# Loading and transposing the first k and q by chunks of 128 tokens, with the opening of a fused attention and FFN kernel reordered

## The chip, the cores and the metric

The kernel runs on one core of a Trainium2 chip. The metric is device time in microseconds (us), the median of several runs. A core has five engines with queues of their own: TensorE (PE; its weight loads are listed as PEld), VectorE (DVE), ScalarE (ACT), GpSimd (POOL) and SyncE (SP). They meet only at semaphores. SyncE, ScalarE and GpSimd can each issue DMAs; GpSimd's go through a queue of their own kind (software descriptors), which here also casts float32 to bfloat16 on the way.

## The reference

Sliding-window causal attention (window 64, 8 batches, 8 heads, 576 tokens, head size 64), its heads put side by side to a 4608 x 512 matrix x, and a gated FFN on it:

```python
scores = (1.0 / np.sqrt(D)) * np.matmul(q, k.transpose(0, 1, 3, 2))
rel = pos[:, None] - pos[None, :]
mask = (rel >= 0) & (rel < 64)
attn = softmax(np.where(mask, scores, -1e9))
x = np.matmul(attn, v)              # -> (B*S, H*D) = (4608, 512)
g = x @ w_gate                      # 512 -> 1536
out = (g * sigmoid(g)) * (x @ w_val) @ w_out   # 1536 -> 512
```

Inputs and output are float32; the kernel works in bfloat16 with float32 accumulation.

## The kernel before

The 4608 tokens are cut into 36 chunks of 128. Attention goes by chunk, the FFN by groups of four chunks (512 tokens): `F` computes tiles of 128 of the 1536 hidden columns (matmuls with Wg, a tanh on ScalarE, matmuls with Wv, two VectorE instructions), `O` multiplies by w_out and stores. Attention of later chunks is threaded between the FFN's matmuls. The order of all work is written out by hand in `build`; a small graph class turns reads and writes of named tiles into semaphore waits, and every engine runs its instructions in the order in which `build` names them.

Only the opening is touched: chunks 0 to 3, which nothing can hide.

- `first_loads` (L801) loads k and q of chunks 0 and 1 together (256 tokens) as float32. Partition p holds, for one of four pairs of heads and one group of eight tokens, 2 KB per head of the pair. Each tensor takes two DMAs, one for the even heads (e0 = 0, from SyncE) and one for the odd (e0 = 1, from ScalarE), each 256 KB over all 128 partitions.
- `first_cast` (through `copy`, L260 on ScalarE, L261 on VectorE) casts to bfloat16, by halves e0.
- `first_T` (L827; L825 for chunks 2 and 3) transposes on TensorE, eight transposes for one tensor, into one PSUM bank. `first_ev` copies one chunk out of that bank into kT or qT.
- `next_load` (L808, GpSimd) loads k or q of chunks 2 and 3 with a cast; it is gated on VectorE's `init_nmask` (L304). `load` (L330) loads v of one chunk, `load_w` (L345) columns of Wg or Wv; `W(a, b)` calls it for both.
- `warm` (L847) runs dummy float32 matmuls on a zeroed tile `wz`, which VectorE sets first (L264).
- `Sa`/`Sbias` (L420) puts the additive mask of a chunk into two PSUM banks, `So` (L439) adds the scores and takes the exponentials on ScalarE (L447, two per chunk). `AVa`/`AVs` (L607) is the product with v, `AVn` (L623, L626) the division by the row sums on VectorE. `Xp` (L784) transposes the result on TensorE and, called with an engine, copies it to xT. `shift` makes copies of v moved by 64 partitions.
- `Fp` (L888 matmuls, L869 tanh, L874 and L876 VectorE) is `F` in steps; its first call takes tokens 0 to 255, so it needs xT of chunks 0 and 1.

PSUM banks are given out least recently used first (`bank`, `pair`).

Of the kernel before, what the change touches and what calls it, by code (L numbers as in the profile page):

```python
# [17 lines left out]
BF = dt.bfloat16  # L18
F32 = dt.float32
# [134 lines left out]
class _Kernel:  # L154
# [111 lines left out]
    def init(self):  # L266
        g = self.g
        self.zero(self.tri[:, :], ["tri"], 1.0)
        self.zero(self.wz[:, :], ["wz"])
        self.zero(self.ident[:, :], ["ident"])  # L270
        self.zero(self.wup[:, :], ["wup"])
        self.zero(self.qT[:, :, 128 * self.ZQ:], ["qpad"])
# [1 line left out]
        t = self.tri  # L274
# [500 lines left out]
    def Xp(self, n, kind="a"):  # L775
# [16 lines left out]

        return ev

    def first_loads(self):
        for x, src in (("k", self.k), ("q", self.q)):
            f, fkeys, _, _ = self.first[x]
            for e0, eng in ((0, "sp"), (1, "act")):
                a = src[0, e0::2, 0:256, :].rearrange("c (g j) d -> g c (j d)", j=8)
                d = f[:, e0].rearrange("p j d -> p (j d)")  # L800
                self.g.op(eng, lambda e, d=d, a=a: e.dma_start(d, a), reads=fkeys, writes=[("f", x, e0)], dma=True)  # L801

    def next_load(self, x, st=1, gate=None):
        d, keys = self.first[x, 1]
# [2 lines left out]
        d = d.rearrange("p j e d -> p e j d").rearrange("p e j d -> p e (j d)")  # L807
        self.g.op("pool", lambda e: e.dma_start(d, a), writes=keys, dma=True, after=gate)  # L808

    def first_cast(self, x, parts):  # L810
        f, fkeys, c, ckeys = self.first[x]
        for e0, j0, j1, eng in parts:
            self.copy(eng, c[:, j0:j1, e0, :], f[:, e0, j0:j1, :], [("f", x, e0)] + fkeys, [("fc", x, e0, j0)])
            self.first[x, 0] = self.first.get((x, 0), []) + [("fc", x, e0, j0)]

    def first_T(self, x, st=0):
        c, ckeys = self.first[x, 1] if st else (self.first[x][2], self.first[x][3] + self.first[x, 0])
        bank, bk = self.bank("a")
        tb = bank.bitcast(BF).rearrange("p (j t) -> p j t", j=8)

        def pe(e):
            for j in range(8):
                if st:
                    for p in range(2):
                        r = e.transpose(tb[64 * p:64 * p + 64, j, :], c[:, j, p, :], self.ident[:, :])  # L825
                else:
                    r = e.transpose(tb[:, j, :], c[:, j, :, :], self.ident[:, :])  # L827
            return r

        self.g.op("pe", pe, reads=["ident"] + ckeys, writes=[bk])  # L830
        return bank, bk

    def first_ev(self, x, n, eng, b, after=None):
        bank, bk = b
        dst = self.kT if x == "k" else self.qT
        g = 16 * (n % 2)
        a = bank.bitcast(BF).rearrange("p (j g c) -> p c g j", j=8, c=4)[:, :, g:g + 16, :]
        d = dst[:, :, 128 * n:128 * n + 128].rearrange("p c (g j) -> p c g j", j=8)
        return self.copy(eng, d, a, [bk], [(x + "T", n, 0), (x + "T", n, 1)], after)

    def warm(self, count):
        bank, bk = self.bank("a")
        z = self.wz[:, :].bitcast(F32)

        def pe(e):
            for _ in range(count):
                r = e.matmul(bank[:, 0:224], z[:, 0:128], z[:, 0:224], start=True, stop=True)  # L847
            return r

        self.g.op("pe", pe, reads=["wz"], writes=[bk])  # L850

    def Fp(self, c, fs, lo=0, hi=512, side=False):
        g = self.g
# [109 lines left out]
    def loads(self):  # L963
# [56 lines left out]
    def build(self):  # L1020
# [4 lines left out]
        self.warm(5)  # L1025
        self.first_cast("k", ((0, 0, 8, "dve"), (1, 0, 8, "act")))
        self.first_cast("q", ((0, 0, 8, "dve"), (1, 0, 5, "dve"), (1, 5, 8, "act")))
        fk = self.first_T("k")
        self.first_ev("k", 0, "dve", fk)
        fq = self.first_T("q")  # L1030
        q0 = self.first_ev("q", 0, "act", fq)
        s0 = self.Sa(0, True)
        self.first_ev("k", 1, "dve", fk)
        self.first_ev("q", 1, "dve", fq, q0)
        s1 = self.Sa(1, True)
        self.So(s0)
        fk = self.first_T("k", 1)
        self.first_ev("k", 2, "dve", fk)
        self.So(s1)
        self.first_ev("k", 3, "dve", fk)  # L1040
        s2 = self.Sa(2, True)
        fq = self.first_T("q", 1)
        self.first_ev("q", 2, "act", fq)
        self.first_ev("q", 3, "act", fq)
        self.early_loads()
        s3 = self.Sa(3, True)
        a0 = self.AVa(0)
        self.AVs(a0)
        self.So(s2)
        self.shift(1, 0, "dve")  # L1050
        self.shift(1, 1, "dve")
        self.AVn(a0)
        a1 = self.AVa(1)
        self.AVs(a1)
        self.So(s3)
        x0 = self.Xp(0)
        self.AVn(a1)
        a2 = self.AVa(2)
        self.AVs(a2)
        self.AVn(a2)  # L1060
        x0("act")
        x1 = self.Xp(1)
        x1("act")
        a3 = self.AVa(3)
        self.AVs(a3)
        x2 = self.Xp(2)
        f0 = self.Fp(0, (0, 1), 0, 256)
        f0("Wg", 0)
        f0("Wg", 1)
        x2("act")  # L1070
        self.AVn(a3)
        x3 = self.Xp(3)
        f0("tan", 0)
        x3("dve")
# [20 lines left out]
        fk = self.first_T("k", 1)  # L1095
        self.held.add(fk[1][1])
        fq = self.first_T("q", 1)
# [61 lines left out]
        for c in range(2, NFC):  # L1159
            for u in range(4):  # L1160
                n = 4 * c + u + 4
# [78 lines left out]
```

## Time and profile before

| | us |
|---|---|
| median of 3 runs | 326.02 (325.84 to 326.12) |
| the profiled execution, its own time | 326.52 |
| its span | 324.8 |
| PE busy | 319.2 (98% of the span) |
| DVE, ACT, POOL busy | 215.8, 125.8, 104.2 |
| DMA traffic | 39.83 MB moved, mean 123 GB/s |

The profile is of one execution. The span runs from its first instruction to its last; the time of an execution is 1.7 us longer. Times in the timeline and in the chain of waits are counted from the span's start. Line numbers are those of the kernel before. In a timeline row the bracket gives the idle time of the engine ahead of the row and what ended it; rows of one line that follow each other are merged, with their count. The DMA view gives for each issue the median time from issue to landing.

### The profile page before, as it was taken

How to read it: one execution, taken by the hardware profiler on the slowest of the kernel's cores; microseconds unless marked ns; L12 is line 12 of the kernel's file. 1: busy time of each engine (PE TensorE's matmuls, PEld its weight loads, DVE VectorE, ACT ScalarE, POOL GpSimd, SP SyncE). 2: the span in 40 equal slices, each digit the busy share in tenths (PEclk: the TensorE clock that was granted, in tenths of full speed). 3: DMA queues.
4: the chain of work that ended last, by engine and by line, in shares of the span. 5: the costliest groups of instructions: out<-in, count | busy, mean ns of one | idle time of the engine just before them, and what ended most of it. 6: DMA issues, size and time to landing. Idle time of an engine off the chain costs nothing.

```text
span 324.8 us, 7717 instructions
## 1 busy us (share of the span) xinstructions
PE 319.2 (98%) x3278; PEld 162.4 (50%) x3278; DVE 215.8 (66%) x400; ACT 125.8 (39%) x224; POOL 104.2 (32%) x134
## 2 busy tenths in 40 slices
PE   6999999999999999999999999999999999999996
PEld 5665565564544454545454444545454544444444
DVE  5886866688485966676768585958576767555510
ACT  3935563634332443333333242424242422222311
POOL 6999831142626061607060607060402000000000
DMA  7999999999999899959998998999687202000012
GB/s 189 179 191 186 205 172 167 161 150 149 158 138 167 128 100 137 163 109 152 119 115 122 146 141 81 146 132 163 71 110 96 69 32 67 32 34 32 32 67 97
DMA packets 154354, 39.83 MB, mean 123 GB/s; under 512 B 140368, under 2 KB 149328, under 8 KB 154320
## 3 DMA queue, kind: packets, MB, share of 16 engines
q0 software_dynamic: 104896, 18.36, 72.8%
q1 hardware_dynamic: 43952, 11.15, 24.7%
q10 hardware_dynamic: 5472, 9.83, 9.5%
q8 instruction: 26, 0.43, 0.5%
q14 instruction: 8, 0.07, 0.1%
HBM read 37.75 MB, written 9.44 MB: 145 GB/s over the span
## 4 chain that ended last, share of the span: by engine, by line
PE 96%; DMA 1%; ACT 1%; DVE 0%; SPq 0%; issue 0%
PE ps L888 58%; PE ps L930 29%; PE ps L692 2%; PE ps L514 2%; DMA hT<-in_q_dram 1%; PE ps L464 1%; PE ps L825 1%; ACT pt L447 1%; PE ps L382 1%; PE ps L420 1%; PE ps L582 1%; PE ps L468 0%; DVE ost L261 0%; PE ps L784 0%; PE ps L439 0%; ACT xT L260 0%
## 5 line engine op out<-in xcount | busy, mean ns | idle before, releaser
L874 DVE SCALAR_TENSOR_TENSOR uu<-sig,ps 128x512 bf16<-128x512 bf16 x108 | 73.9, 685 | 57.3 <-ACT sig L869 57.1
L888 PE MATMUL ps<-xT,Wg 128*128 128x512 bf16 (+1 forms) x456 | 111.2, 369 | 0.1
L888 PE MATMUL ps<-xT,Wv 128*128 128x512 bf16 (+1 forms) x456 | 111.0, 368 | 0.0
L869 ACT ACTIVATE sig<-ps 128x512 bf16<-128x512 f32 x108 | 65.1, 603 | 89.0 <-PE ps L888 89.0
L930 PE MATMUL ps<-Wo,hT 128*128 128x512 bf16 (+1 forms) x444 | 98.8, 374 | 0.0
L876 DVE SCALAR_TENSOR_TENSOR hT<-uu,ps 128x512 bf16<-128x512 bf16 x108 | 74.2, 687 | 3.7
L888 PEld LDWEIGHTS ps<-xT,Wv 128*128 128x128 bf16 x456 | 44.5, 98 | 48.4
L930 PEld LDWEIGHTS ps<-Wo,hT 128*128 128x128 bf16 x444 | 43.3, 98 | 49.2
L888 PEld LDWEIGHTS ps<-xT,Wg 128*128 128x128 bf16 x456 | 42.7, 98 | 45.5 <-ACT xT L260 0.6
L330 POOL DMA_DIRECT2D kn<-in_k_dram x29 | 24.9, 861 | 107.7 <-PE ps L888 103.7
L330 POOL DMA_DIRECT2D va<-in_v_dram x40 | 34.4, 889 | 34.0 <-PE ps L888 34.0
L260 ACT ACTIVATE ost<-ps 128x512 f32<-128x512 f32 (+1 forms) x22 | 12.9, 587 | 52.9 <-PE ps L930 52.9
L261 DVE COPY ost<-ps 128x512 f32<-128x512 f32 (+1 forms) x15 | 10.1, 674 | 30.1 <-PE ps L930 30.1
L524 ACT ACTIVATE pt<-ps 128x512 bf16<-128x512 f32 x36 | 18.6, 603 | 29.0 <-PE ps L514 29.0
L330 POOL DMA_DIRECT2D qn<-in_q_dram x29 | 25.1, 870 | 0.3 <-issue 0.3
L476 ACT ACTIVATE pt<-ps 128x512 bf16<-128x512 f32 x28 | 14.5, 603 | 12.9 <-PE ps L468 12.9
L727 DVE TENSOR_TENSOR xb<-ps,rc 128x512 bf16<-128x512 f32 (+2 forms) x39 | 18.8, 510 | 0.5
L692 PE MATMUL ps<-va,pt 64*64 64x65 bf16 x800 | 12.3, 192 | 0.0
L490 DVE TENSOR_TENSOR pt<-pt,kmask 128x1024 bf16<-128x1024 bf16 x18 | 11.5, 683 | 0.0
L692 PEld LDWEIGHTS ps<-va,pt 64*64 64x64 bf16 x800 | 10.3, 107 | 0.0
L723 DVE RECIPROCAL rc<-ps 128x8 f32<-128x8 f32 (+2 forms) x39 | 5.7, 174 | 6.5 <-PE ps L692 6.5
L490 DVE TENSOR_TENSOR pt<-pt,mask 128x1024 bf16<-128x1024 bf16 x14 | 9.3, 686 | 0.9 <-ACT pt L476 0.8
(76 smaller groups left out, 131.6 us busy)
## 6 DMA issues: line engine op xcount, KB each, us to landing
out_dram<-ost ACTq DMA_DIRECT2D x35, 256.0 KB, 2.9
va<-in_v_dram POOLq DMA_DIRECT2D x32, 128.0 KB, 5.5
kn<-in_k_dram POOLq DMA_DIRECT2D x23, 128.0 KB, 4.2
qn<-in_q_dram POOLq DMA_DIRECT2D x23, 128.0 KB, 4.5
Wg<-in_moe_w_gate_dram POOLq DMA_DIRECT2D x6, 256.0 KB, 6.6
Wv<-in_moe_w_val_dram POOLq DMA_DIRECT2D x6, 256.0 KB, 7.4
Wo<-in_moe_w_out_dram POOLq DMA_DIRECT2D x2, 768.0 KB, 15.3
ks<-in_k_dram POOLq DMA_DIRECT2D x2, 256.0 KB, 7.1
```

The source lines that it names most:

```text
L260: return self.g.op("act", lambda e: e.activation(d, a, ACTF.Copy), reads=reads, writes=writes, after=after)
L330: self.g.op("pool", lambda e, d=d, a=a: e.dma_start(d, a), writes=ks, dma=True, after=gate)
L476: g.op("act", lambda e, po=po, p=p: e.activation(po, sv[p], ACTF.Exp, scale=SCALE), reads=[bx[p][1]], writes=[pk[p]])
L490: self.g.op("dve", lambda e: e.tensor_tensor(pt, pt, m, ALU.mult), reads=pk + mk, writes=pk)
L524: g.op("act", lambda e, po=po, p=p: e.activation(po, sv[p], ACTF.Exp, scale=SCALE), reads=[bx[p][1]], writes=[pk[p]])
L692: x = e.matmul(o, ab[0], ab[1], start=first, stop=phase == 1, skip_group_check=True)
L727: g.op("dve", lambda e, av=av, hs=hs, w=w, rc=rc, xo=xo: e.tensor_tensor(xo[:, :, hs, :], av[:, :, :, 0:64], rc[:, :, hs].unsqueeze(3).to_ ...
L869: g.op("act", lambda e: e.activation(sig[:, 0:w], G[:, 0:w], ACTF.Tanh, scale=0.5), reads=[gk], writes=[("sig", i)])
L874: g.op("dve", lambda e: e.scalar_tensor_tensor(uu[:, 0:w], sig[:, 0:w], 1.0, G[:, 0:w], ALU.add, ALU.mult), reads=[("sig", i), gk], writes ...
L876: g.op("dve", lambda e: e.scalar_tensor_tensor(out, v3(uu), 0.5, v3(V), ALU.mult, ALU.mult), reads=[("uu", i), vk], writes=[("hT", ih, f) ...
L888: r = e.matmul(bank[:, a * n:a * n + n], W[:, kk, f * 128:f * 128 + 128], xT[:, kk, lo:hi], start=(kk == 0), stop=(kk == NK - 1))
L930: r = e.matmul(OB[:, 0:n], hT[:, f, 128 * u:128 * u + 128], self.Wo[:, f, lo:hi], start=(f == 0), stop=(f == NF - 1))
```

## The change

- `first_loads` now makes six DMAs. Chunk 0 first, with k and q each by even heads (SyncE) and odd heads (ScalarE), 128 KB over 64 partitions (0 to 63); then chunk 1's k and q, each as a whole, 256 KB over partitions 64 to 127, both on SyncE.
- Casts, transposes and evictions go by chunk. The transposes of chunks 0 and 1 take 64 rows each, so there are four groups of eight instead of two.
- GpSimd issues v of chunk 0 between k and q of chunks 2 and 3.
- The dummy matmuls read a constant zero, broadcast, instead of the tile `wz`, which goes with its memset; there are 3 of 328 columns instead of 5 of 224.
- `build` is reordered up to the first FFN matmuls: the product with v of chunk 0 goes ahead of the scores of chunk 1, the transpose of chunk 0's result goes ahead of the transposes of q of chunks 2 and 3, and that of chunk 2's result behind the first Wg matmuls. The order after that is the same.

The diff, cut to its core:

```diff
-        self.wz = sb("wz", 512)
-        self.zero(self.wz[:, :], ["wz"])
+    def first_load(self, x, n, es, eng):
+        src = (self.k if x == "k" else self.q)[0, :, 128 * n:128 * n + 128, :]
+        f, fkeys, _, _ = self.first[x]
+        f = f[64 * n:64 * n + 64]
+        if len(es) == 2:
+            a = src.rearrange("(c e) (g j) d -> g c e (j d)", e=2, j=8)
+            d = f.rearrange("p e j d -> p e (j d)")
+        else:
+            a = src[es[0]::2].rearrange("c (g j) d -> g c (j d)", j=8)
+            d = f[:, es[0]].rearrange("p j d -> p (j d)")
+        self.g.op(eng, lambda e: e.dma_start(d, a), reads=fkeys, writes=[("f", x, n, e0) for e0 in es], dma=True)
+
     def first_loads(self):
-        for x, src in (("k", self.k), ("q", self.q)):
-            f, fkeys, _, _ = self.first[x]
-            for e0, eng in ((0, "sp"), (1, "act")):
-                a = src[0, e0::2, 0:256, :].rearrange("c (g j) d -> g c (j d)", j=8)
...
+        for x in "kq":
+            self.first_load(x, 0, (0,), "sp")
+            self.first_load(x, 0, (1,), "act")
+        for x in "kq":
+            self.first_load(x, 1, (0, 1), "sp")
...
+    def first_cast(self, x, n, e0, eng):
+        f, fkeys, c, ckeys = self.first[x]
+        rows = slice(64 * n, 64 * n + 64)
+        self.copy(eng, c[rows, :, e0, :], f[rows, e0], [("f", x, n, e0)] + fkeys, [("fc", x, n, e0)])
...
-                    r = e.transpose(tb[:, j, :], c[:, j, :, :], self.ident[:, :])
+                    r = e.transpose(tb[:, j, :], c[rows, j, :, :], self.ident[rows, rows])
...
-    def warm(self, count):
+    def warm(self, count, n):
         bank, bk = self.bank("a")
-        z = self.wz[:, :].bitcast(F32)
+        zero = self.nc.const_aps.tensor_like(0.0, bank[:, 0:n])
...
-                r = e.matmul(bank[:, 0:224], z[:, 0:128], z[:, 0:224], start=True, stop=True)
+                r = e.matmul(bank[:, 0:n], zero[:, 0:128], zero, start=True, stop=True)
...
         self.next_load("k", gate=done)
+        self.load(0, "v")
         self.next_load("q")
-        for n in range(4):
-            self.load(n, "v")
-        self.W(0, 2)
+        self.load(1, "v")
+        self.load(2, "v")
+        self.load(3, "v")
+        self.load_w("g", 0, 2)
+        self.load_w("v", 0, 2)
```

The opening in `build`, after the change:

```python
self.warm(3, 328)
self.first_cast("k", 0, 0, "dve")
self.first_cast("k", 0, 1, "act")
self.first_cast("q", 0, 0, "dve")
self.first_cast("q", 0, 1, "act")
fk = self.first_T("k", 0, 0)
self.first_ev("k", 0, "dve", fk)
fq = self.first_T("q", 0, 0)
self.first_cast("k", 1, 1, "act")
self.first_ev("q", 0, "act", fq)
self.first_cast("k", 1, 0, "dve")
s0 = self.Sa(0, True)
gk = self.first_T("k", 0, 1)
self.So(s0)
self.first_cast("q", 1, 0, "dve")
self.first_cast("q", 1, 1, "dve")
self.first_ev("k", 1, "dve", gk)
gq = self.first_T("q", 0, 1)
self.first_ev("q", 1, "dve", gq)
s1 = self.Sa(1, True)
a0 = self.AVa(0); self.AVs(a0); self.AVn(a0)
self.So(s1)
fk2 = self.first_T("k", 1)
k2 = self.first_ev("k", 2, "dve", fk2)
self.first_ev("k", 3, "dve", fk2)
s2 = self.Sa(2, True)
x0 = self.Xp(0)
fq2 = self.first_T("q", 1)
x0("act")
q2 = self.first_ev("q", 2, "act", fq2)
self.first_ev("q", 3, "act", fq2)
self.early_loads()
self.shift(1, 0, "dve"); self.shift(1, 1, "dve")
s3 = self.Sa(3, True)
self.So(s2)
a1 = self.AVa(1); self.AVs(a1); self.AVn(a1)
self.So(s3)
a2 = self.AVa(2); self.AVs(a2)
x1 = self.Xp(1)
self.AVn(a2)
x1("act")
a3 = self.AVa(3); self.AVs(a3); self.AVn(a3)
f0 = self.Fp(0, (0, 1), 0, 256)
f0("Wg", 0); f0("Wg", 1)
x2 = self.Xp(2)
x2("act")
x3 = self.Xp(3)
f0("tan", 0)
x3("dve")
```

More of the change, by code (lines that the diff above doesn't have):

```diff
@@ L808, in next_load, with first_T @@
         self.g.op("pool", lambda e: e.dma_start(d, a), writes=keys, dma=True, after=gate)
-    def first_cast(self, x, parts):
+    def first_cast(self, x, n, e0, eng):
         f, fkeys, c, ckeys = self.first[x]
[L812 to L817, printed above, removed]
-        bank, bk = self.bank("a")
-        tb = bank.bitcast(BF).rearrange("p (j t) -> p j t", j=8)
+        rows = slice(64 * n, 64 * n + 64)
+        self.copy(eng, c[rows, :, e0, :], f[rows, e0], [("f", x, n, e0)] + fkeys, [("fc", x, n, e0)])
+    def first_T(self, x, st, n=0):
+        bank, bk = self.bank("a")
+        if st:
+            c, ckeys = self.first[x, 1]
+            tb = bank.bitcast(BF).rearrange("p (j t) -> p j t", j=8)
+        else:
+            c, ckeys = self.first[x][2], self.first[x][3] + [("fc", x, n, e0) for e0 in range(2)]
+            tb = bank.bitcast(BF)[:, 0:512].rearrange("p (j t) -> p j t", j=8)
+        rows = slice(64 * n, 64 * n + 64)
         def pe(e):
@@ L835, in first_ev @@
         dst = self.kT if x == "k" else self.qT
-        g = 16 * (n % 2)
-        a = bank.bitcast(BF).rearrange("p (j g c) -> p c g j", j=8, c=4)[:, :, g:g + 16, :]
+        if n < 2:
+            a = bank.bitcast(BF)[:, 0:512].rearrange("p (j g c) -> p c g j", j=8, c=4)
+        else:
+            g = 16 * (n % 2)
+            a = bank.bitcast(BF).rearrange("p (j g c) -> p c g j", j=8, c=4)[:, :, g:g + 16, :]
         d = dst[:, :, 128 * n:128 * n + 128].rearrange("p c (g j) -> p c g j", j=8)
         return self.copy(eng, d, a, [bk], [(x + "T", n, 0), (x + "T", n, 1)], after)
-    def warm(self, count):
+    def warm(self, count, n):
         bank, bk = self.bank("a")
-        z = self.wz[:, :].bitcast(F32)
+        zero = self.nc.const_aps.tensor_like(0.0, bank[:, 0:n])
         def pe(e):
             for _ in range(count):
-                r = e.matmul(bank[:, 0:224], z[:, 0:128], z[:, 0:224], start=True, stop=True)
+                r = e.matmul(bank[:, 0:n], zero[:, 0:128], zero, start=True, stop=True)
             return r
-        self.g.op("pe", pe, reads=["wz"], writes=[bk])
+        self.g.op("pe", pe, writes=[bk])
     def Fp(self, c, fs, lo=0, hi=512, side=False):
@@ L1047, in build @@
         a0 = self.AVa(0)
         self.AVs(a0)
-        self.So(s2)
+        self.AVn(a0)
+        self.So(s1)
+        fk2 = self.first_T("k", 1)
+        k2 = self.first_ev("k", 2, "dve", fk2)
+        self.first_ev("k", 3, "dve", fk2)
+        s2 = self.Sa(2, True)
+        x0 = self.Xp(0)
+        fq2 = self.first_T("q", 1)
+        x0("act")
+        q2 = self.first_ev("q", 2, "act", fq2)
+        self.first_ev("q", 3, "act", fq2)
+        self.early_loads()
         self.shift(1, 0, "dve")
@@ L1051, in build @@
         self.shift(1, 1, "dve")
-        self.AVn(a0)
+        s3 = self.Sa(3, True)
+        self.So(s2)
         a1 = self.AVa(1)
         self.AVs(a1)
+        self.AVn(a1)
         self.So(s3)
-        x0 = self.Xp(0)
-        self.AVn(a1)
         a2 = self.AVa(2)
         self.AVs(a2)
+        x1 = self.Xp(1)
         self.AVn(a2)
-        x0("act")
-        x1 = self.Xp(1)
         x1("act")
@@ L1065, in build @@
         self.AVs(a3)
-        x2 = self.Xp(2)
+        self.AVn(a3)
         f0 = self.Fp(0, (0, 1), 0, 256)
@@ L1069, in build @@
         f0("Wg", 1)
+        x2 = self.Xp(2)
         x2("act")
[L1071 removed]
         x3 = self.Xp(3)
```

22 lines of the change are left out of this document (1 added, 21 removed).

## The prediction

> **What bounds the kernel now.** I read the page first, then the chain of waits in order of time, then the timeline of the opening, the busy time by stage, and the DMA issues with their time to landing.
>
> The page says where the time is:
>
> ```profile
> span 324.8 us, 7717 instructions
> PE 96%; DMA 1%; ACT 1%; DVE 0%; SPq 0%; issue 0%
> ```
>
> TensorE carries 96% of the chain; the other 4% lies at the two ends. The profiled run took 326.52 us, 1.7 us around its span, and the median of the three runs is 326.02. I work out a difference against the profiled span and put it on the median. About 0.2% (0.65 us) is what a measurement of this kernel can tell from no change.
>
> The chain in the opening (start, length, what):
>
> ```profile
> 0.81 0.66 SPq L801
> 1.47 0.06 issue
> 1.53 4.83 DMA hT<-in_q_dram
> ...
> 7.56 0.61 PE ps L827 x8
> ...
> 9.36 0.57 PE ps L825 x16
> 9.93 0.34 PE ps L439 x16
> 10.27 0.54 PE ps L420 x2
> 10.81 0.57 PE ps L825 x16
> ...
> 11.91 0.24 PE ps L607 x8
> ...
> 12.54 2.06 ACT pt L447 x4
> ...
> 15.63 1.05 PE ps L888 x8
> 16.68 0.22 PE ps L784 x4
> 16.91 11.25 PE ps L888 x64
> ```
>
> Three links: the first q load until 6.4; TensorE's scores, biases and transposes until about 12; then ScalarE until the first FFN matmul at 15.63. From 16.91 on TensorE is solid, and the rest of the program is untouched. So the change is worth what it moves that solid block, and no more. On ScalarE, VectorE, TensorE and GpSimd the same stretch reads (start, length, engine, line, operation):
>
> ```profile
> 1.08 0.27 DVE L264 MEMSET wz<- 128x256 uint32 x1
> ...
> 1.40 4.10 PE L847 MATMUL ps<-wz 128*128 128x224 f32 x10 [1.40 <-DVE wz L264]
> ...
> 3.31 0.83 POOL L808 DMA_DIRECT2D ks<-in_k_dram  x1 [1.46 <-DVE nmask L304]
> ...
> 4.14 0.71 POOL L808 DMA_DIRECT2D qs<-in_q_dram  x1
> 4.78 0.63 ACT L260 ACTIVATE ost<-hT 128x512 bf16<-128x512 f32 x1 [1.14 <-DMA hT<-in_k_dram]
> 4.85 3.67 POOL L330 DMA_DIRECT2D va<-in_v_dram  x4
> 5.00 0.43 DVE L261 CAST ost<-hT 128x512 bf16<-128x512 f32 x1 [1.30 <-DMA hT<-in_k_dram]
> ...
> 5.52 1.01 PE L827 MATMUL ps<-ident,ost 128*128 128x128 bf16 x8
> ...
> 7.34 1.27 DVE L261 COPY kT<-ps 128x512 bf16<-128x512 bf16 x2
> ...
> 8.48 0.79 POOL L345 DMA_DIRECT2D Wg<-in_moe_w_gate_dram  x1
> ...
> 9.40 2.06 ACT L447 ACTIVATE pt<-ps 128x512 bf16<-128x512 f32 x4 [0.60 <-PE ps L439]
> ...
> 11.41 1.08 ACT L260 ACTIVATE qT<-ps 128x512 bf16<-128x512 bf16 x2
> ...
> 14.46 1.72 ACT L260 ACTIVATE xT<-ps 128x512 bf16<-128x512 bf16 x3
> ```
>
> ScalarE has no gap from 9.40 to the eviction that releases the FFN: four exponentials, two q evictions, four exponentials, two x evictions. To be earlier, its whole sequence must start earlier or lose a member.
>
> **The loads: the term that decides.** Busy time by stage (edges; length; busy PE, PEld, DVE, ACT, POOL; clock; DMA share; GB/s):
>
> ```profile
> 2.20:3.10 0.90, 0.90 (x4) 0.78 (x4) 0.76 (x5) 0.90 (x1) 0.00 (x0) 1.00 0.75 109
> 3.10:4.25 1.15, 1.15 (x5) 1.03 (x4) 0.60 (x5) 0.53 (x2) 0.94 (x2) 1.00 1.01 388
> 4.25:5.00 0.75, 0.75 (x4) 0.59 (x2) 0.00 (x1) 0.22 (x1) 0.75 (x2) 1.00 1.08 407
> 5.00:5.75 0.75, 0.73 (x5) 0.26 (x4) 0.42 (x1) 0.41 (x1) 0.75 (x1) 1.00 1.02 306
> ```
>
> The first 0.90 us brings 0.10 MB, then the flow is flat at 388 to 407 GB/s with all 16 engines occupied (share 1.01 to 1.08). The k load of both chunks is 0.524 MB, so it is in at 3.10 + (0.524 - 0.098)/0.388 = 4.20; ScalarE starts on it at 4.78 (0.58 later) and VectorE at 5.00 (0.80 later). I use these two delays below.
>
> Before, every such load fills 128 partitions. After, each of the six fills 64: k and q of chunk 0 go to partitions 0 to 63 (four DMAs of 0.131 MB), k and q of chunk 1 to 64 to 127 (two of 0.262 MB, behind the others on SyncE's queue; SyncE issues four at 0.66 each, so the last is out by about 3.5, which limits nothing). No row shows a hardware-queue load of 64 partitions. Bounds: at the row's rate (half the bytes, half the time), or at half that rate, if the flat ceiling is the write side's and belongs to the partitions. Faster than the row's rate I exclude: the engines are already occupied.
>
> - At the full rate: chunk 0's k is in at 3.10 + (0.262 - 0.098)/0.388 = 3.5, its q at 4.2, chunk 1's k at 4.8, its q at 5.5.
> - At half: k 3.10 + 0.164/0.194 = 3.95, then 0.262/0.2035 = 1.29 each: q 5.2, k 6.5, q 7.8.
>
> GpSimd's k load shares the engines from about 5, which I allow up to 0.6 for: q of chunk 1 at 5.5 to 6.1, or 7.8 to 8.4.
>
> I take the slow end. The nearest row is a 128-partition one and would say the fast end; but its rate does not move when one queue drains after another, and a ceiling of that kind looks to me more like one of lanes than of single transfers. It is a judgement, at 5 to 4. The Trainium skill speaks against this change here: SBUF — State Buffer, section "Door 1: The DMA port swizzle (why `[64,N]` ≈ `[32,N]`)", says that partitions 0 to 63 reach only 8 of the 16 ports, and measures 196 GB/s there against 328 on all 128; by it the sum is that of the slow end, and no run here shows it yet.
>
> **Forecast, step by step.** With chunk 1's q in at 7.8 to 8.4, VectorE sees it at 8.6 to 9.2. It has by then cast and evicted what came earlier. It needs two casts at 0.43, and two evictions at 0.64 (half of 1.27), with the transposes of q beside the first: 2.14, so chunk 1's q stands transposed at 10.75 to 11.35. Ahead of it on ScalarE, the cast of half of chunk 1's k (now queued before the eviction of chunk 0's q) waits until 6.5 + 0.6, so the q eviction, and the scores of chunk 0 behind it, come at about 8.5 to 9, no sooner than before.
>
> Then TensorE, in the new order: scores of chunk 1 0.34, transposes of k 0.57, bias 0.54, the x transposes of chunk 0 0.22, transposes of q 0.57: 2.24, to 13.0 to 13.6. Then ScalarE without a gap: two q evictions 1.08, four exponentials 2.06, one x eviction 1.72/3 = 0.57: 3.71. The other x eviction has gone into the gap before, which spares 0.57. With 0.1 for hand-overs the FFN starts at 16.8 to 17.4, against 15.63: 1.2 to 1.8 later. And x transposes of two chunks instead of one now stand between the first Wg matmuls and the solid block (before, the other one lay in TensorE's wait): 0.22 more. **Sum: 1.4 to 2.0 later; I say 1.8, as GpSimd's sharing lies at the late end. 326.0 + 1.8 = 327.8 us.**
>
> The small parts:
> - Dummies: TensorE waited until 1.40 for the memset; now it starts near 0.9 (an estimate: SyncE's first instruction is at 0.81) and runs 3 x 328 instead of 5 x 224 columns, 4.10 x 984/1120 = 3.6, to 4.5. The first transposes come at 5.2 in the forecast, so nothing is added; without that cover it would be worth at most 0.5.
> - The memset gone (0.27) brings GpSimd's gate on nmask up to 0.27 forward; it has waited for that. Its queue then runs the same DMAs.
> - V of chunk 0 ahead of q. Issue and landing (KB each, us):
>
> ```profile
> ks<-in_k_dram POOLq DMA_DIRECT2D x1, 256.0 KB, 4.1
> qs<-in_q_dram POOLq DMA_DIRECT2D x1, 256.0 KB, 5.4
> va<-in_v_dram POOLq DMA_DIRECT2D x1, 128.0 KB, 5.5
> Wg<-in_moe_w_gate_dram POOLq DMA_DIRECT2D x1, 256.0 KB, 5.8
> ```
>
> k landed at 7.4, q at 9.5, V 0 at 4.85 + 5.5 = 10.35. V 0 then lands at about 8.3 to 8.6, and q takes its place at 10.35, up to 0.26 earlier for the earlier gate or some 2 later if the first loads hold the engines. Its transposes are due at 12.5 in the forecast: covered, with nothing left over. At the full rate they are due near 10.4 and q is next to late.
> - Wg 0, 1 land at 8.48 + 5.8 = 14.3, 1.3 ahead of their use; pushed by up to 2, they still make 16.8.
>
> **Rivals.**
> 1. *Full rate, and it comes to almost nothing.* Chunk 1's q is seen at 6.3 to 6.9, transposed at 8.45 to 9.05; V 0 lets its attention product (0.24) run by 8.9. Scores of chunk 1 at 8.9 to 9.1, transposes of q done by 11.15 to 11.35, FFN at 14.95 to 15.15, less 0.22: 0.25 to 0.45 gained, 325.6 to 325.8. For it: the same 2 KB rows, queues and engines as in the rows above. Against: the ceiling. 22%.
> 2. *Full rate, and the wait is GpSimd's q alone.* If everything before it is in time, the q transposes start on the landing, 10.1 to 10.35, and end by 10.7 to 10.9: FFN at 14.5 to 14.7, 0.7 to 0.9 gained after the 0.22: 325.2. It is the most that the order allows. 20%.
> 3. *Slower still: the clock.* The same eight transposes took 1.01 at 5.52 and 0.61 at 7.56, though the granted clock reads 1.00 throughout: TensorE was slow until after 6.5, behind 5 us of unbroken work. The new opening has gaps after 4.5. If it does not get up to speed, the 2.24 become 2.24 x 1.01/0.61 = 3.7, and the first FFN work runs slow as well until the clock comes up: 2 to 3 more in all, 330 to 331 on the forecast, 328 to 329 on the fast loads. It decides once the gaps are too long to count as work, which no row tells. 8%.
>
> **How the numbers follow.** Forecast 50%, all of it slower. Rival 1 22%, of which 2% may pass the bound to faster; rival 2 20%, faster; rival 3 8%, slower. Faster 0.22, same 0.20, slower 0.58. The forecast's own range is 327.2 to 328.4. The whole range reaches down to rival 2's centre and up past the forecast's late end, 325.2 to 328.8; outside lie the better half of rival 2 and most of rival 3.
>
> **What would show it.** Right: while the first loads run, about 200 GB/s instead of 388 to 407; ScalarE's first cast near 4.6 as before, chunk 1's q cast on VectorE after 8.6; first exponential near 9, a gap on ScalarE between the second and third pair; first Wg matmul at 16.8 to 17.4. Wrong: 390 GB/s in the first loads, first cast near 4.1, first exponential before 8; then rivals 1 and 2 part by whether the q transposes of chunks 2, 3 wait for TensorE's own queue or for the landing. Transposes and biases at double length after 7.5 would be rival 3. A wait on weights after the FFN's start would be none of these.

## The result and the profile after

| us | before | after |
|---|---|---|
| median of 4 runs | 326.07 (325.84 to 326.35) | 330.13 (329.53 to 330.81) |
| the profiled execution | 326.52 | 330.81 |
| its span | 324.8 | 329.1 |
| first FFN matmul starts | 15.63 | 19.74 |
| solid block starts | 16.91 | 21.24 |

The change makes the kernel slower: ratio 1.0125, 95% interval 1.01 to 1.0149, or 4.06 us between the medians. The forecast was 327.8 with a range up to 328.8. The direction was right, the size less than half.

In the page's line on the chain TensorE had 96% before:

```profile
PE 92%; DMA 2%; ACT 2%; issue 1%; DVE 1%; SPq 1%
```

The shares are not the measure of the loss: this profile lists 878 of the 912 FFN matmuls with Wg and Wv, and the missing ones leave gaps that count as "issue". The opening is read in times.

The chain of waits in the opening, after (start, length, what):

```profile
3.07 5.94 DMA hT<-in_q_dram
...
9.03 0.98 DVE ost L260 x2
...
10.05 0.60 PE ps L840 x8
10.66 0.97 PE ps L418 x2
11.63 0.44 PE ps L605 x8
12.07 0.54 PE ps L437 x11
12.60 1.00 PE ps L838 x16
13.60 0.97 PE ps L418 x2
14.57 0.43 PE ps L782 x4
14.99 1.01 PE ps L838 x15
16.03 1.09 ACT qT L259 x2
...
17.14 2.06 ACT pt L445 x4
19.20 0.50 ACT xT L259
...
19.74 1.05 PE ps L904 x8
20.79 0.45 PE ps L782 x8
21.24 2.62 PE ps L904 x24
```

It has the links that the prediction named: chunk 1's q (until 9.03), TensorE's queue, ScalarE, the FFN. Two links grew. The load ends 2.6 us later than the q load did before (6.39). And the TensorE steps between 10.7 and 16 take nearly double: two biases 0.97 instead of 0.54, sixteen transposes 1.00 instead of 0.57, the x transposes 0.43 instead of 0.22.

Busy time by stage while the first loads run (edges; length; busy PE, PEld, DVE, ACT, POOL; clock; DMA share; GB/s):

```profile
3.10:4.25 1.15, 1.15 (x3) 0.34 (x1) 0.42 (x4) 1.13 (x3) 1.11 (x2) 1.00 0.93 205
4.25:6.00 1.75, 0.80 (x9) 0.45 (x8) 1.06 (x2) 0.52 (x1) 1.75 (x3) 1.00 0.95 215
```

That is the half rate: 205 and 215 GB/s where 388 and 407 stood, with the DMA engines still as busy (share 0.93 to 0.95). Each engine is occupied, but with slower transfers: the median piece of 2 KB that starts between 3.1 and 5 takes 84 ns before and 135 to 138 ns after.

The timeline of TensorE and VectorE, after:

```profile
0.85 3.62 PE L863 MATMUL ps<-const-float32-0.0 128*128 128x328 f32 x6 [0.85 <-PEq L1252]
...
5.22 0.58 PE L840 MATMUL ps<-ident,ost 64*128 64x64 bf16 x8 [0.75 <-issue]
...
9.03 0.97 DVE L260 CAST ost<-hT 64x512 bf16<-64x512 f32 x2 [1.71 <-DMA hT<-in_q_dram]
...
12.54 1.07 PE L838 MATMUL ps<-ident,ks 128*64 128x128 bf16 x16
...
15.92 0.61 PE L418 MATMUL ps<-nmask,ident 128*128 128x512 bf16 x2
```

The dummies end at 4.47 and the first transposes come 0.75 later. The k transposes of chunks 2 and 3 take 1.07 (0.64 before); only from the biases at 15.92 on is it at full rate (0.61, as two biases took at 10.20 before). The granted clock reads 1.00 in every stage of this profile. So a clock column of 1.00 doesn't mean full speed here. The trace's records of the granted clock say why: the first of them starts at 15.96, and the column counts a stretch without a record as 1.00. Ahead of it the slow phase is seen only by setting the same operation beside itself.

Of the signs that the prediction named, the half rate, the first exponential (8.89) and the q cast (9.03) came as forecast. ScalarE's first cast came at 3.62, not near 4.6: it needs only the odd heads of chunk 0's k, one of the DMAs, and follows ScalarE's work ahead of it without a wait.

### The profile page after: what moved, and what is told of

Same layout as the page of the kernel before. It is cut to its first block, busy times and chain, and to the rows that moved or that the text cites. A ratio compares the mean times of both kernels' runs of the same rounds, so it can differ in the third digit from the quotient of the medians.

```text
span 329.1 us, 7705 instructions
## 1 busy us (share of the span) xinstructions
PE 318.1 (97%) x3251; PEld 163.1 (50%) x3290; DVE 217.0 (66%) x401; ACT 126.9 (39%) x225; POOL 104.7 (32%) x134
## 4 chain that ended last, share of the span: by engine, by line
PE 92%; DMA 2%; ACT 2%; issue 1%; DVE 1%; SPq 1%
PE ps L904 55%; PE ps L946 28%; PE ps L690 2%; DMA hT<-in_q_dram 2%; PE ps L512 2%; PE ps L838 1%; PE ps L462 1%; SPq L803 1%; ACT pt L474 1%; ACT pt L445 1%; PE ps L380 1%; PE ps L418 1%; PE ps L782 1%; DVE ost L260 0%; DVE uu L890 0%
## 5 line engine op out<-in xcount | busy, mean ns | idle before, releaser
L904 PE MATMUL ps<-xT,Wg 128*128 128x512 bf16 (+1 forms) x436 | 106.6, 367 | 3.0 <-issue 2.7
L259 ACT ACTIVATE ost<-ps 128x512 f32<-128x512 f32 (+1 forms) x22 | 12.9, 588 | 52.9 <-PE ps L946 52.9
L474 ACT ACTIVATE pt<-ps 128x512 bf16<-128x512 f32 x28 | 14.5, 602 | 12.9 <-PE ps L466 12.9
```

Of the source, the lines that this page charges most:

```text
L259: return self.g.op("act", lambda e: e.activation(d, a, ACTF.Copy), reads=reads, writes=writes, after=after)
L474: g.op("act", lambda e, po=po, p=p: e.activation(po, sv[p], ACTF.Exp, scale=SCALE), reads=[bx[p][1]], writes=[pk[p]])
L904: r = e.matmul(bank[:, a * n:a * n + n], W[:, kk, f * 128:f * 128 + 128], xT[:, kk, lo:hi], start=(kk == 0), stop=(kk == NK - 1))
```

## The experiments

The theory after the result: the loss has two parts, the half rate of the loads (chunk 1's q later) and the half rate of TensorE, which the wait for that q brings about. Rivals: the new order itself costs the time; or one of the two parts is all of it. Ratios are against the kernel before on the same chip, whose medians there were 326.27 to 326.67.

### The loads by themselves

`m1_loads` leaves out all computation. Seven stages follow each other, each of four DMAs of 256 KB, two from SyncE and two from ScalarE; only the place in SBUF changes: all 128 partitions, 0 to 63, 32 to 95, 64 to 127, both halves at once (SyncE into 0 to 63, ScalarE into 64 to 127), one chunk over all 128 in rows of 1 KB, and the first again.

> Leaves out everything but loads: seven stages of four DMAs of 256 KB from the tensors of this kernel, two each from SyncE and ScalarE, each stage after the last has landed; only the rate of each stage counts. Stage 1 and 7: the loads of the kernel before (128 partitions, 256 tokens). Stage 2: 64 partitions, 0 to 63, one chunk per DMA (the change's form). Stage 3: 64 partitions, 32 to 95. Stage 4: 64 to 127. Stage 5: SyncE on 0 to 63 and ScalarE on 64 to 127 at once. Stage 6: one chunk per DMA as in stage 2, but over 128 partitions in rows of 1 KB. Theory (which partitions are written decides, 0 to 63 and 64 to 127 each have half of the ways): about 390 GB/s in 1, 3 and 7, about 200 to 220 in 2 and 4, 200 to 250 in 5 as two engines that share a way work in step; 6 above 300. Rival (64 partitions are slow wherever they lie): 3 as slow as 2. Second rival (reading one chunk of 128 tokens is slow, the write side is not): 6 as slow as 2.

Busy time by stage of `m1_loads`, one window inside each of its stages (edges; length; busy POOL; clock; DMA share; GB/s):

```profile
3.00:5.00 2.00, 0.00 (x0) 1.00 1.06 406
8.50:11.50 3.00, 0.00 (x0) 1.00 1.08 220
16.00:18.00 2.00, 0.00 (x0) 1.00 1.02 381
22.00:25.00 3.00, 0.00 (x0) 1.00 1.05 206
29.50:32.00 2.50, 0.00 (x0) 1.00 1.06 230
36.00:37.80 1.80, 0.00 (x0) 1.00 1.07 365
42.30:44.00 1.70, 0.00 (x0) 1.00 1.05 401
```

64 partitions are not the cause, but which 64: 32 to 95 take 381 GB/s, 0 to 63 take 220, 64 to 127 take 206. Filling both halves at once gives 230, hardly more than one. The Trainium skill's SBUF — State Buffer, sections "Door 1: The DMA port swizzle (why `[64,N]` ≈ `[32,N]`)" and "Can I just issue two DMAs to hit both halves?", has it so: the partition's bit of 64 picks between two sets of 8 ports, so a range within one half reaches 8 of 16, and two transfers on the two halves gain 6%. These rows agree, the range across the middle too.

`e8_before_new_loads` is the kernel before with the change's six DMAs and nothing else:

```diff
-        for x, src in (("k", self.k), ("q", self.q)):
-            ...
-                self.g.op(eng, lambda e, d=d, a=a: e.dma_start(d, a), reads=fkeys, writes=[("f", x, e0)], dma=True)
+        for x in "kq":
+            self.first_load(x, 0, (0,), "sp")
+            self.first_load(x, 0, (1,), "act")
+        for x in "kq":
+            self.first_load(x, 1, (0, 1), "sp")
```

> The kernel before with the change's six first loads alone; the casts wait for both chunks' loads, all else is as before (dummies 1.40 to 5.5). Theory (64-partition loads take 2.4 us more for the four tensors' halves): k is cast near 7.3, q near 8.8 instead of 6.4, the FFN starts 2.2 to 2.6 later, 328.3 to 329; where the gap in TensorE's work leaves it at half rate, 330 to 331. Rival (chunk 0 lands early enough that the load form alone costs little): below 327.3.

330.35 us (329.92 to 330.95), ratio 1.0118 (1.009 to 1.0146): the loads alone cost as much as the whole change. Its chain of waits:

```profile
8.81 0.97 DVE ost L261 x2
...
9.92 1.01 PE ps L838 x8
10.93 1.71 PE ps L420 x4
...
19.24 1.05 PE ps L899 x8
```

The FFN starts 3.61 later than before. The q casts start 2.42 later (8.81 against 6.39); behind that wait the transposes of q take 1.01 instead of 0.61 and the four biases 1.71 instead of 0.86, 1.25 together. 2.42 + 1.25 = 3.67: both parts are there, without the new order. Here TensorE had come up (the transposes of k at 7.85 took 0.61) and fell back.

`e2_old_loads` is the opposite: the change with the four DMAs of before (the diff above, turned round).

> The changed kernel with the first loads of the kernel before (four DMAs of 256 KB over 128 partitions, two chunks each); casts, transposes, order and dummies stay those of the change. Theory (64-partition loads are one cost, the rate of TensorE another): the loads run at about 390 GB/s again, q of chunk 1 is cast from 6.4, and the 2 us of the loads are back; if TensorE stays at half rate, 328 to 329, if denser work also brings it up, 325.5 to 326.2. Rival (the loads cost nothing, the time is all in TensorE's rate): within 0.5 of the changed kernel, 330.

328.96 us (328.21 to 329.49), ratio 1.0069 (1.0052 to 1.0086). The loads run at 378 GB/s again, yet it is still 2.3 slower than before. In its chain TensorE's steps are long:

```profile
7.27 0.97 PE ps L418 x2
...
11.58 0.99 PE ps L839 x16
...
17.84 1.05 PE ps L905 x8
```

So TensorE's half rate doesn't need the slow loads; the rest of the change suffices. It is a part of its own.

### Can the half rate be mended, and who else uses the engines?

`e3_halves` puts k and q of one chunk into opposite halves, k from SyncE and q from ScalarE:

```diff
+    def half(self, x, n):
+        m = (n + (x == "q")) % 2
+        return slice(64 * m, 64 * m + 64)
...
+        for x, eng in (("k", "sp"), ("q", "act")):
+            for e0 in range(2):
+                self.first_load(x, 0, (e0,), eng)
+        for x, eng in (("k", "sp"), ("q", "act")):
+            self.first_load(x, 1, (0, 1), eng)
```

> The changed kernel with the same six 64-partition DMAs of the same sizes, but k and q in opposite halves: chunk 0's k in partitions 0 to 63 from SyncE and its q in 64 to 127 from ScalarE, chunk 1's the other way round (1 DMA each from SyncE and ScalarE). Theory (the ceiling belongs to the partitions that are written, so two halves together have all of it): about 390 GB/s from 3.1 on, k and q of chunk 0 both in at about 4.2, those of chunk 1 at 5.5 to 6, time 1.5 to 2 below the changed kernel: 328 to 328.6 if TensorE stays at half rate, 325.4 to 326 if not. Rival (a DMA on 64 partitions is slow in itself, whichever they are): about 200 GB/s, q of chunk 1 cast near 9, 330.

330.7 us (329.1 to 331.4), ratio 1.0117 (1.0088 to 1.0145), 233 to 239 GB/s from 3.1 on. My expectation that both halves at once fill the engines fell; the fifth stage of `m1_loads` says the same.

`d1_pool_gated` (with five dummies) holds GpSimd's first load until chunk 1's q has landed; everything of GpSimd's then comes late, so only the landing counts:

```diff
+        rd = [("f", "q", 1, 0)] if gate is not None else []
-        self.g.op("pool", lambda e: e.dma_start(d, a), writes=keys, dma=True, after=gate)
+        self.g.op("pool", lambda e: e.dma_start(d, a), reads=rd, writes=keys, dma=True, after=gate)
```

> The changed kernel with 5 dummies, and GpSimd's first load (and so all behind it) held until chunk 1's q has landed. Only the landing counts; all that follows comes later. Theory (half of the ways carries about 205 GB/s, and GpSimd's load, which shares the engines from 5 on, adds the rest): q of chunk 1 cast at 8.0 to 8.3 instead of 9.0. Rival (GpSimd's sharing costs nothing): at 9.0 as in the changed kernel. Second rival (the sharing is all of it): before 7.2.

The chain of waits gives the q load 4.67 instead of 5.94, to 7.73:

```profile
3.06 4.67 DMA hT<-in_q_dram
```

Sharing with GpSimd's loads of k, v and q costs chunk 1's q 1.3 us in the change (its cast starts at 9.03, here at 7.75) and 0.4 in the profiled run of `e1_warm5` below (8.19); the prediction allowed up to 0.6. The kernel as a whole took 333.11 in its one run, held by v. The 7.73 fits the prediction's 7.8 for the half rate without sharing, and the cast follows 0.02 behind it, not 0.8.

### TensorE's rate

`e1_warm5` is the change with five dummies of 328 columns instead of three, which fill TensorE until the first transposes:

```diff
-        self.warm(3, 328)
+        self.warm(5, 328)
```

> The changed kernel with 5 dummy matmuls of 328 columns instead of 3; nothing else. They run from 0.85 to about 6.9 instead of 4.5. Theory (two costs: slow first loads, and TensorE left at half rate because work is broken off after 4.5): TensorE gets up to speed near 7, transposes and biases after 10 take 0.6 instead of 1.05, the first Wg matmul comes at about 17.4 and the time is 327.8 +- 0.5. Rival (the gaps that the slow loads leave keep the rate down whatever the dummies do): half rate until about 16 as in the changed kernel, 330 to 331.

Nine runs, median 329.5, ratio 1.0069 (1.0046 to 1.0092), and they fall into two groups: 327.41, 327.75, 327.88, 327.94, all with a mean granted clock of 1.000; and 329.5, 329.88, 329.88, 329.91, 330.15, with 0.994 to 0.995. The profile is of the 327.75 run. `e1b_warm5` is the same kernel once more, and its profile is of a 330.16 run (clock 0.995).

> The changed kernel with 5 dummies once more, for one more profile: of nine runs four took 327.4 to 327.9 and five 329.5 to 330.2. Theory (the moment at which TensorE changes its rate is not tied to the program): either 327.4 to 328 with all work after 7.5 at full rate, or 329.5 to 330.2 with a stretch of 3 to 4 us at half rate in the opening or at the FFN's start. Rival (the two groups are two states of the DMAs): both with TensorE at full rate, the slow one with later landings.

The timeline of TensorE, first in the 327.75 run, then in the 330.16 run:

```profile
9.01 0.40 PE L840 MATMUL ps<-ident,ost 64*128 64x64 bf16 x8 [0.31 <-DVE ost L260]
...
11.99 0.64 PE L838 MATMUL ps<-ident,qs 128*64 128x128 bf16 x16
```

```profile
10.10 0.40 PE L840 MATMUL ps<-ident,ost 64*128 64x64 bf16 x8 [1.73 <-DVE ost L260]
...
11.76 1.06 PE L838 MATMUL ps<-ident,ks 128*64 128x128 bf16 x16
...
14.14 1.06 PE L838 MATMUL ps<-ident,qs 128*64 128x128 bf16 x16
```

In the first, TensorE waits 0.31 for chunk 1's q and keeps its rate. In the second q comes 0.85 later (cast at 9.04 instead of 8.19), TensorE waits 1.73, and soon after it the rate falls. This time the stages of the 330.16 run show it in the clock column (the last but two):

```profile
8.00:11.00 3.00, 1.27 (x23) 0.81 (x23) 1.93 (x4) 1.09 (x2) 2.66 (x4) 1.00 1.75 174
11.00:14.00 3.00, 2.87 (x47) 1.91 (x44) 2.36 (x5) 1.09 (x2) 2.04 (x4) 0.62 2.07 170
14.00:17.00 3.00, 2.84 (x68) 1.84 (x66) 1.30 (x5) 2.33 (x5) 2.90 (x5) 0.81 1.46 197
```

TensorE is busy 1.27 of 3.0 us from 8 to 11, and granted 0.62 from 11 to 14. The FFN starts at 16.62 in the one and 18.96 in the other: 2.34, of which q's landing explains 1.09 (10.10 against 9.01) and the rate the rest. Why q lands 0.85 earlier in one run isn't known.

The records of the granted clock in the traces (us from the span's start):

| profiled run | full rate from | half from | full again from |
|---|---|---|---|
| the change | 15.96 | | |
| `e2_old_loads` | 12.91 | | |
| `e3_halves` | 16.11 | | |
| `e1_warm5` | 5.99 | | |
| `e1b_warm5` | 4.90 | 11.72 | 15.14 |
| `e8_before_new_loads` | 5.76 | 9.18 | 12.59 |
| `e4_before_dummies` (below) | 4.64 | | |

So the half rate has two forms. In the change, `e2` and `e3`, with three dummies, TensorE comes up only at 12.9 to 16.1; in `e1b` and `e8` it comes up and falls back behind a wait. Each stretch between two records is 3.41 us long or a multiple of it: 3.41, 6.83, and 314.03, which is 92 times 3.41. Against the program the edges lie elsewhere in each execution. A mean clock of 0.995 is one such stretch at half rate (half of 3.41 in 328 us). The Trainium skill's TensorE: Matmul & The Clock Gate, section "Part 1: The HAM clock gate (the "warmup" mystery)", puts the rate down to a monitor that sees activity in windows of 3.4 us, which don't start with the kernel; the records agree. How much of a window must be filled isn't shown.

`d2_fill` keeps TensorE at work in the wait: five dummies at the start, three behind the scores of chunk 0, one ahead of the product with v of chunk 0.

```diff
         self.So(s0)
+        self.warm(3, 328)
...
+        self.warm(1, 328)
         a0 = self.AVa(0); self.AVs(a0); self.AVn(a0)
```

> The changed kernel with 5 dummies at the start and four more in TensorE's waits (three of 328 columns behind the scores of chunk 0, one ahead of its product with v); loads and order of the change. Theory (waiting for chunk 1's q is what drops TensorE to half rate about 11 to 14): the group of runs at 329.5 to 330.2 that 5 dummies alone left is gone, all runs at 327.4 to 328.2, granted clock 1.00 in every stage. Rival (the rate drops at random, work or not): two groups as before, about half of the runs above 329.

329.4 us (329.2 to 329.96), ratio 1.0096 (1.0079 to 1.0113), clock 1.00 in all runs: one group. (The trace of the profiled run has no clock record; there the durations tell.) But the fillers stand in the way. The chain of waits:

```profile
9.11 1.86 PE ps L863 x6
10.97 0.34 PE ps L840 x8
11.31 0.54 PE ps L418 x2
11.85 0.55 PE ps L863 x2
12.40 0.24 PE ps L605 x8
...
18.63 1.05 PE ps L904 x8
```

The q casts end at 9.92, the transposes start at 10.97 in the chain: 1.0 lost, and 0.55 for the second filler. Every step of the change's work is at full rate (0.34, 0.54, 0.24). Without the 1.55 the FFN would start at 17.1 and the time be 327.9, with q as late (8.92) as in the change. That difference is worked out, not run.

### With both parts mended, is there a gain?

`e4_before_dummies` and `e6_before_warm4` are the kernel before with the constant-zero dummies, three and four of 328 columns; `f2_before_warm4` is the latter again.

```diff
-        self.warm(5)
+        self.warm(3, 328)
```

> The kernel before with the change's dummies alone (3 of 328 columns on the constant zero, no wz, no memset); loads and order of before. Theory (TensorE needs unbroken work beyond 4.5 to get up to speed): the transposes of k start at 5.5 after a gap of 1 us, TensorE stays at half rate until after 10 or so, 327.5 to 329. Rival (in the changed kernel it is the later gaps that matter): transposes and biases after 7.5 at full rate as before, 326.0 +- 0.3.

> The kernel before with the constant-zero dummies, 4 of 328 columns (0.85 to about 5.3). Theory (unbroken work up to the first transposes is what brings TensorE up to speed, and an earlier start helps): 325.8 to 326.5, no wider spread than before. Rival (the length of the dummies does not matter, the constant operand or the missing memset does): 327.3 as with 3 of them.

> The kernel before with 4 dummies on the constant zero once more, beside the last one on the same chip: 326.2 to 326.6, granted clock 1.00. Theory (an unbroken start of TensorE settles its rate): spread no wider than that of the kernel before.

Three: 327.27 (326.35 to 328.47), ratio 1.0025 (1.001 to 1.004). Four: 326.43 (325.8 to 326.78), 0.999 (0.9975 to 1.0005), and 326.25, 0.9998 (0.9984 to 1.0012). So in the old order three dummies are 0.6 to 0.8 slower than the kernel before, and four are as good as it. That the three cost this by the rate is argued, not shown: the profile of `e4` is of its fastest run (326.35), in which TensorE was at full rate from 4.64 and did the transposes of k in 0.62. There the same three dummies that leave the change at half rate were enough.

The FFN starts at 14.70 in the profiled run of `e4` and at 14.73 in that of `e6` (326.08), 0.9 earlier than before, and that is hardly seen in the time. The timeline of `e4`:

```profile
5.34 0.62 PE L825 MATMUL ps<-ident,ost 128*128 128x128 bf16 x8 [0.88 <-ACT ost L259]
...
14.70 1.05 PE L886 MATMUL ps<-xT,Wg 128*128 128x256 bf16 x8
...
16.51 1.05 PE L886 MATMUL ps<-xT,Wv 128*128 128x256 bf16 x8 [0.54 <-DMA Wv<-in_moe_w_val_dram]
```

The next matmuls wait for the first Wv. In `e6` they don't: its solid block starts at 16.00, 0.91 earlier than before, yet its span is only 0.4 shorter. At 48 us 0.59 of the 0.91 is left; what takes the rest isn't shown.

`f1_shifts_first` puts GpSimd's copies of v among the second pair of weight loads, on top of four dummies: one copy ahead of Wg 2, 3 and two ahead of Wv 2, 3. It came out slower, 328.42, ratio 1.0049 (1.003 to 1.0068). Three of its eight runs took 326.97 to 327.21, five 328.38 to 329.03; the profile is of the 326.97 run. There GpSimd waits 1.03 for v ahead of the moved copy of v 2, until 11.32, the copies end at 13.99 and the FFN starts at 14.90. What the five slower runs lost isn't shown.

> The kernel before with 4 dummies on the constant zero, and on GpSimd the moved copy of v 2 ahead of the loads of Wg 2, 3 and the other two copies ahead of Wv 2, 3 (before: both loads first). With 4 dummies alone the chain led through GpSimd's queue to 13.8 and the FFN started at 14.7. Theory (GpSimd's queue is what binds once TensorE and the loads are in order): the copies end at about 13.2, the FFN starts at 14.2 to 14.6, 325.6 to 326.2. Rival (the landing of Wv, near 16, binds already, or the later loads give it back): no difference to 326.4.

`e5_old_loads_warm5` and `e7_old_loads_warm4` are the change with the old loads and five or four dummies: the new order alone, with TensorE kept busy.

> The changed kernel with the loads of before and 5 dummies of 328 columns; order, casts and transposes by chunk, and v 0 ahead of q stay. Theory (the loads and TensorE's rate are the two costs and nothing else of the change costs): 326 to 326.8 in runs at full rate, no better than before because the first Wv then waits for its landing near 16.4; up to 2 more where the rate drops. Rival (the order or the work by chunk costs by itself): 327.5 or more even at full rate.

> The changed kernel with the loads of before and 4 dummies of 328 columns: what is left of the change is casts, transposes and evictions by chunk, the new order, v 0 ahead of q. With 5 dummies this took 327.5 at full rate, its chain led through the dummies until 6.3. Theory (the dummies alone held it up): transposes of k at 5.4, FFN at 15.4, 326.5 +- 0.3. Rival (order and work by chunk cost 0.5 to 1 themselves): 327.2 to 327.7 at full rate.

Five: 327.5 (327.16 to 327.94), ratio 1.0018 (1.0005 to 1.0031), at full rate; its chain begins on the dummies, then VectorE's queue:

```profile
0.85 5.47 PE ps L864 x10
...
7.39 1.52 DVE ost L260 x3
```

Four: 328.55, ratio 1.0058 (1.0033 to 1.0083), spread from 327.14 to 329.92; the profiled run (328.23) was at half rate from 8.82 to 12.24 by its clock records, and its FFN started at 17.11. Even the best single run, 327.14, is no gain. Whether the order and the work by chunk cost something by themselves stays open: 327.5 is what that rival forecast, but with five dummies the chain leads through them until 6.32, and with four the profiled run lost its rate. No version that was run beats the kernel before.

### Chunk loads over all partitions

`c1_full_rows` keeps the change's order and loads each chunk over 128 partitions, a row then being four tokens (1 KB); `c2_full_rows_old_order` does the same in the old order from the scores of chunk 1 on, and `c3_full_rows_two_queues` also sends chunk 1's q from ScalarE.

```diff
-        f = f[64 * n:64 * n + 64]
+        f = f[:, :, 4 * n:4 * n + 4, :]
-            a = src[es[0]::2].rearrange("c (g j) d -> g c (j d)", j=8)
+            a = src[es[0]::2].rearrange("c (g j) d -> g c (j d)", j=4)
```

> The change with its loads by chunk spread over all 128 partitions (rows of 4 tokens, 1 KB, instead of 8 tokens, 2 KB; the casts take half as many elements per partition, four transposes of 128 instead of eight of 64) and 4 dummies. Theory (the chunk was never the trouble, the half of the partitions was): loads at 355 to 370 GB/s, chunk 1's q cast before 6.3, all at full rate, FFN at 14.8 to 15.3, then the landing of Wv near 16 decides: 325.8 to 326.4, at best as fast as the kernel before. Rival (the order by chunk costs in itself): 327 or more.

> As the last (loads by chunk over 128 partitions, 4 dummies), but from the scores of chunk 1 on in the order of the kernel before, with q of chunks 2 and 3 ahead of v 0. Theory (with the loads whole, what bounds the opening is GpSimd's queue and the landing of the first Wg, Wv): 325.6 to 326.3, within 0.2% of the kernel before. Rival (the earlier first transposes carry through): 325.3 or less.

> The kernel with loads by chunk over 128 partitions (1 KB rows), 4 dummies and the old order, with chunk 1's q issued from ScalarE instead of SyncE. With both on SyncE the first loads ran at 200 to 255 GB/s and q was cast at 9.4, although no transfer took longer than on 128 partitions (46 ns per 1 KB). Theory (one queue of 1 KB rows does not fill the engines): 350 GB/s from 3.1 to 5, q cast near 6.5, 326 to 327. Rival (GpSimd's load, not the queue, holds the last transfers): q cast after 8, 328 or more.

330.0 (ratio 1.01, 1.0073 to 1.0128), 329.01 (1.0073, 1.0047 to 1.01) and 327.94 (1.0057, 1.004 to 1.0074). The stages of `c1_full_rows`:

```profile
3.10:4.25 1.15, 1.15 (x3) 0.67 (x2) 0.63 (x5) 1.06 (x3) 1.10 (x2) 1.00 0.89 238
4.25:5.75 1.50, 1.50 (x7) 0.85 (x5) 0.29 (x1) 0.00 (x0) 1.50 (x3) 1.00 0.89 273
```

238 to 273 GB/s, though the sixth stage of `m1_loads` ran such rows at 365. There all four DMAs were of 256 KB and nothing else ran; which of the differences matters is open. The first two times hold a loss of rate as well: in the profiled runs TensorE waits 1.78 and 1.58 us for chunk 1's q and is at half rate from 9.20 to 16.03 and from 10.67 to 14.08. In that of `c3_full_rows_two_queues` it keeps its rate. With q on the other queue the casts of chunk 1 come before 8.3 instead of 9.4, the best of the chunked loads, and the chain then runs through GpSimd's queue, which waits for v until 11.92.

## Why the prediction was right and wrong

- **The loads: right.** Half the rate was taken, 200 GB/s; 205 and 215 were measured, and `m1_loads` shows it to be the partitions'. Chunk 1's q was forecast on VectorE at 8.6 to 9.2 and came at 9.03. That the moment was met is luck: two errors cancel. The allowance for GpSimd's sharing (up to 0.6) was too small, as `d1_pool_gated` against the change shows 1.3. And the 0.8 that was added for VectorE is no delay of VectorE: it lies between a landing worked out from bytes and the cast, while the chain in the prediction has the q load end at 6.36 and the cast start at 6.39. Without sharing the cast started at 7.75, where 7.8 + 0.8 would have been the forecast.
- **TensorE's stretch: wrong, and this is the step that failed.** The forecast priced it at the rate that the profile of before shows after 7.5, 2.24 us, and left the wait's effect on that rate out. From 9.03 its terms give 9.03 + 2.14 + 2.24 + 3.71 + 0.1 = 17.2 for the FFN; it started at 19.74. The q eviction ended at 11.39 (10.70 + 0.69) instead of 11.17. TensorE, behind its biases and the product with v at half rate, began the scores of chunk 1 at 12.00, 0.6 later. Then the stretch of 2.24 took 4.0, until 16.03. ScalarE's 3.71 were 3.67. So 2.4 of the 2.5 are the half rate, and 330.1 - 2.4 = 327.7. The four runs of `e1` at full rate took 327.4 to 327.9, with the same loads and order; in the profiled one q came 0.84 earlier than in the change, and Wg then held the FFN by 0.29.
- **Rival 3 had the mechanism and the price, not the chance.** "2 to 3 more in all, 330 to 331 on the forecast, 328 to 329 on the fast loads": 330.13 was measured, and 328.96 with the old loads. It was given 8%, as a case beside the forecast. It was a consequence of it: the forecast itself had TensorE idle from the end of the dummies at 4.5 until 5.2, and again until chunk 1's q. The row for the slow transposes at 5.52, behind 4.1 us of unbroken work, stood in the prediction; it said that in that run even a longer stretch of work had not been enough. `e4`, at full rate behind 3.6 us of it, shows that the length alone doesn't decide.
- **"Nothing is added" for the dummies: wrong.** Their cover was looked for in the time that they take, not in what they do for the rate. Two more of them in the change bring the first full rate from 15.96 to 5.99 and 4.90 in the two profiles. In the old order three cost 0.6 to 0.8, by a cause that no profile shows.
- **Rivals 1 and 2 could not come about in full.** The prediction followed the landing of Wg (14.3, "pushed by up to 2") and not that of Wv. In `e4` Wv holds the second group of matmuls at 16.51 while the FFN starts at 14.70; in the 327.75 run of `e1` the Wg landing, at 16.48, holds the FFN by 0.29. Nor is a start at 14.70 or 14.73 worth the 0.7 to 0.9 that rival 2 gave it: the profiled spans of `e4` and `e6` are 0.2 and 0.4 shorter than that of before, and in `e6` no landing accounts for the difference.
- **The small terms.** The solid block starts 1.50 behind the FFN, 1.28 before: the 0.22 for the second x transpose was right. V of chunk 0 ahead of q was covered: no row of the chain names that q.

## What to carry to other kernels

When an edit makes the engine that bounds the kernel wait longer, ask at once whether that engine keeps its rate through the wait: set the same operation beside itself in the profile, and don't rely on the clock column, which reads 1.00 wherever the trace has no record. A load cut into pieces should be costed by the partitions that each piece fills, and by what else moves at that moment; a small kernel of loads alone settles it in one run. Where a step is to come earlier, list every landing that is due next, not only the first.

## What the hardware showed that was not expected

- A DMA's rate hangs on which partitions it fills: 32 to 95 at 381 GB/s, 0 to 63 at 220, 64 to 127 at 206, both halves by two queues at once 230.
- TensorE's rate can stay down for the whole opening (the change: 1.07 for what takes 0.64, first record of the full rate at 15.96) or come up and fall back (`e1b_warm5`, half rate from 11.72 to 15.14). One and the same kernel, with five dummies, took 327.4 to 327.9 in four of nine runs and some 2.1 us more in five, those with a stretch at half rate.
- The granted clock changes at edges that are 3.41 us or a multiple apart and lie elsewhere in each execution: with three dummies up to 4.47 the full rate came at 4.64 in `e4` and at 15.96 in the change.
- Rows of 1 KB over all partitions, in pieces of 128 and 256 KB, ran at 238 to 273 GB/s beside other work in `c1_full_rows`, in pieces of 256 KB at 365 by themselves; the cause is open.
